# The first unit of a chunked delta rule: the inverse applied chunk by chunk inside the recurrence, with a new table of ranks

## The chip, the core and the metric

The kernel runs on one core of a Trainium2 chip. The metric is the device time of one execution in microseconds (us); lower is better. The time before is the median of four runs.

## What is computed

The input is a delta rule (linear attention with a correcting update) followed by a mixer. There are B=4 batches, H=8 heads, S=768 steps and head size D=48; everything is float32.

```python
for t in range(S):                      # per batch and head; k_n is k divided by its norm
    y[t]  = q[t] @ state
    state = state + beta[t] * outer(k_n[t], v[t] - k_n[t] @ state)
x = y, heads side by side               # (4, 768, 384)
u = x + (V^T U^T x, along the sequence) # U is 768x32, V is 32x768
out = u + relu(u @ w_ch1) @ w_ch2       # w_ch1 384x1536, w_ch2 1536x384
```

## The kernel before

**Units and chunks.** The sequence is cut into chunks of 64 steps. A unit is half of one batch: six chunks for all eight heads. There are eight units, n = 0 to 7, and batch b owns units 2b and 2b+1. Two large buffers (`slot`) hold alternate units: `kn` (k), `kq` (k and q turned, so that D lies on partitions), `pg` (first the products k k^T, later the inverse, then called `zt`), `qk` (masked q k^T), `vn` (v, in the room that q had) and `kz` (another copy of half of k).

**A unit's steps.** `load` brings k, q, v and z in by DMAs of 72 KB, four for each four heads (L383); v can only be loaded when q of the same unit has been turned, as it takes q's room. `grams` turns k and q on TensorE (L479), copies them out (L494) and forms the products (L506; masks at L537). `norms` takes the root on ScalarE (L445), forms the coefficients on VectorE (L448 to L453), and at L462 multiplies v by the norms, once v has landed. `blocks` inverts the triangular matrices: a transpose (L588), a multiply (L592), a substitution of many short VectorE instructions (L597, L603), a transpose back (L610), and `joins`, small matmuls that put the parts together (L653, L667, L693 to L714, with VectorE at L619 and L671). `diagonals` writes the result into `pg` (L732). `prepare` then forms, for three chunks at a time, (Z K)^T in the place of K^T (L812, copied by ScalarE at L831) and Z v in the place of v (L823, copied at L836). Z is the inverse.

**The recurrence.** `recur(b)` goes through the twelve chunks of a batch in order. For each chunk: TensorE multiplies (Z K) by the state (L861), VectorE subtracts that from Z v, which gives z (L874), TensorE forms K^T z (L889), and VectorE adds it to the state (L899). `outputs` forms q times the state (L776) and adds the masked product with z (L790), and ScalarE copies the result into `X` (L760).

**The mixer.** When all of a batch is in `X`, `front` forms the low-rank part (L1184, L1201) and turns the tokens (L1209). `wide` is the two large products, L1296 for w_ch1 and L1336 for w_ch2, with seven products in the place of eight by the scheme that needs sums of weights and of hidden values (L929, L1259). The last batch's first product is in `quick` (L1089). The weights arrive as pairs of 32-bit words and VectorE converts them in 14 slices, five instructions each (`load_weights`, L993 to L1021), with one ScalarE instruction between (L978).

**The order of the work.** The kernel is written as many generators ("parts"). Each yields its steps one at a time, with the engine and an assumed cost. While the kernel is built, the planner `run` keeps an assumed clock for each engine and takes one step after another; among the steps that could start within a small `hold` of the earliest one, it takes the one with the lowest rank. Each engine's instructions run on the chip in the order so written. The ranks have defaults in the code (recurrence of batch 0: 1; `norms`, `grams` and `blocks` of unit 0: 10, of unit 1: 14; `load_weights`: 40; `wide`: 95), and the table `PLACES` replaces some of them. The ranks were found by a search; they are no property of the computation. The four pairs of PSUM banks (`pair`) are handed out by the planner too, and two of the pairs go over to one bank each for the mixer when batch 0 is nearly done.

A matmul instruction of float32 appears in the profile as two records, so eight matmuls are 16 records.

Of the kernel before, what the change touches and what calls it, by code (L numbers as in the profile page):

```python
# [8 lines left out]
FP32 = mybir.dt.float32  # L9
# [17 lines left out]
def kernel(  # L27
# [20 lines left out]
    nc = tc.nc  # L48
# [61 lines left out]
    def need(*keys):  # L110
        return [key for key in keys if key[1] >= 0]
# [26 lines left out]
            waits[i] = s  # L138

    PLACES = """  # L140
    add_up b1 i0 15.701; block b0 i0 c0 64.5; block b0 i1 c2 71.091; block b0 i1 c3 56.313
    block b0 i2 c5 93.473; block b1 i0 c0 14.618; block b1 i0 c1 14.618; block b1 i1 c2 14.618
    block b1 i1 c3 14.618; block b1 i2 c4 14.618; block b1 i2 c5 14.618; block b2 i0 c0 93.5
    block b2 i0 c1 93.5; block b2 i1 c2 93.5; block b2 i1 c3 93.5; block b3 i0 c0 65.835
    block b3 i0 c1 65.835; block b3 i2 c4 65.835; block b3 i2 c5 65.835; blocks n0 1.5
    blocks n3 97.0; blocks n5 79.5; diagonals n1 h0 59.5; front b1 i0 79.5
    front b2 i0 58.8; gather b0 i0 h1 c0 70.591; gather b0 i1 h1 c0 70.591; gather b0 i1 h1 c1 70.591
    gather b1 i0 h1 c1 79.0; gather b1 i2 h1 c0 97.0; gather b2 i0 h0 c0 21.0; gather b2 i1 h1 c0 21.0
    gather b2 i1 h1 c1 21.0; grams n2 i0 81.482; grams n2 i1 89.482; grams n3 i0 20.0
    grams n5 i0 31.5; grams n5 i1 20.5; grams n7 i0 13.5; joins n1 h0 12.5  # L150
    joins n2 h0 -3.0; joins n2 h1 -3.0; joins n7 h0 106.5; joins n7 h1 102.5
    last_sum b0 i0 74.5; last_sum b2 i0 27.644; load n0 namev halves(0, 1) 74.591; load n1 namek halves(0, 1) 49.32
    load n1 nameq halves(0, 1) 49.32; load n1 namez halves(0, 1) 49.82; load n4 namek halves(0, 1) 86.5; load n7 namek halves(0, 1) 75.587
    load_beta u0 14.5; load_weights 68.5; norms n1 59.3; norms n2 81.804
    norms n7 91.523; outputs b0 c2 3.5; outputs b0 c4 76.5; outputs b0 c6 46.644
    outputs b0 c7 36.586; outputs b0 c9 90.5; outputs b1 c11 9.0; outputs b1 c5 57.185
    outputs b2 c0 37.5; outputs b2 c11 37.5; outputs b2 c5 37.5; outputs b3 c5 79.0
    placed n6 i1 j0 6.5; prepare n2 h1 5.0; prepare n3 h1 37.477; products n0 i0 j1 58
    products n0 i1 j1 58; products n1 i0 j0 81.119; products n2 i0 j1 3.5; products n2 i1 j0 76.0
    products n3 i0 j0 66.5; products n3 i0 j1 21.301; products n4 i1 j0 58.0; products n5 i1 j0 79.5  # L160
    products n5 i1 j1 79.5; products n6 i1 j0 53.243; products n6 i1 j1 70.0; products n7 i1 j0 87.58
    recur b2 46.313; recur b3 72.5; relu b0 i1 60.403; relu b1 i2 23.537
    wide b0 i0 81.619; wide b0 i1 92.619; wide b2 i1 103
    """
    PLACES = dict(x.strip().rsplit(" ", 1) for x in PLACES.replace("\n", ";").split(";") if x.strip())

# [42 lines left out]
    def run():  # L209
        stall = {}  # L210
        while waits or woken:
            while woken:
                i = woken.pop(0)
                at = max([0.0] + [done[x] for x in asked[i]])
                if at > ready[i]:
                    last[i] = None
                advance(i, None, max(at, ready[i]))
            some = {}
            for i, s in waits.items():
                e, was = s["e"], last.get(i)  # L220
# [12 lines left out]
            picks = []  # L233
            for e, them in some.items():
                soon = min(at for at, _ in them)
                them.sort(key=lambda x: (not waits[x[1]]["rush"], x[1]))
                for at, i in them:
                    hold = 0.5 if i[0] < 13 else HOLD if i[0] < 90 else SWITCH
                    if at > soon + hold:
                        continue  # L240
                    if not any(a < at and a + waits[x]["cost"] < at + 0.05 for a, x in them):
                        picks.append((at, i))
                        break
            at, i = min(picks)
            at -= stall[i]
            s, got = waits[i], None
            if s["take"]:
                banks, of = places(s)
                got = min(of, key=lambda y: (banks[y], y))
                del banks[got]  # L250
# [31 lines left out]
    def half(i, size=L):  # L282
        return slice(L * i, L * i + size)
# [81 lines left out]
    def load(n, name, halves):  # L365
# [7 lines left out]
            e = "sp" if halves == (0,) else "act"  # L373
        else:
            e = "sp"
        queue = dict(sp=nc.sync, act=nc.scalar)[e]
        for g in halves:
            if n >= NU and g:
                queue = nc.gpsimd
            for s in range(1, 4, 2) if name == "z" else range(4):  # L380
                to = dict(k=s, q=s, v=s % 2 * 2 + s // 2, z=s // 2)[name]
                yield op(e, 0.65, port=False)
                queue.dma_start(  # L383
                    out=t[half(1 - g if name == "z" else g), :, to, 0:D],
                    in_=src[b, 4 * g + s, hf * UC * L : (hf + 1) * UC * L, :].rearrange(
                        "(c t) d -> t c d", t=L
                    ),
                )
                after = landing(384)
                if name == "z" or s % 2:  # L390
                    emitted((name, n, g, s // 2), after)
# [173 lines left out]
    def blocks(n):  # L565
# [179 lines left out]
        yield need(*[(x, n, h) for x in ("upper", "diagonal") for h in range(2)])  # L745
        emitted(("joined", n))

    def recur(b):
        heads = [(j, par, g) for j in range(2) for par, g in QUADS]
        x = X[:, b % 2]  # L750
# [2 lines left out]
        def states(t):  # L753
            return t.rearrange("p g (j d) -> p g j d", j=2)
# [48 lines left out]
        def prepare(n, h):  # L803

            kn, kq, zt, _, _, vn, _, _ = units[n]
            yield need(("upper", n, h), ("diagonal", n, h), ("grams", n), ("scaled", n))
            cs = range(3 * h, 3 * h + 3)
            x = yield op("pe", 0.7, "Q", take="pair", words=96, flow=0.48)
# [38 lines left out]
        for c in range(NC):  # L847
# [3 lines left out]
            if cu == UC - 1:  # L851
                begin(outputs(c, s_old), 2 if b == 0 else 60)
                yield need(("y1", b, c))
            if c == 0:
                zs[c] = vn[:, cu]
                emitted(("b", b, c))
            else:
                xb = yield op("pe", 0.24, "Q", take="pair", words=32, flow=0.12)
                p_b = pair(xb)[:, :, 0 : 2 * D]
                for j, par, g in heads:  # L860
                    nc.tensor.matmul(  # L861
                        states(p_b)[half(g ^ par), par, j],
                        kq[half(par, D), cu, j, 0, half(g)],
                        states(s_old)[half(par, D), g, j],
                        start=True,
                        stop=True,
                    )
                emitted(("b", b, c))
                if cu < UC - 1:
                    begin(outputs(c, s_old), 2 if b == 0 else 60)  # L870
                yield need(("y", b, c - 3)) if c > 2 else []
                yield op("dve", dve(192), give=[("pair", xb)])
                z = zs[c] = small.tile([128, 4, D], FP32, name="z", bufs=3)
                nc.vector.tensor_tensor(  # L874
                    out=z.rearrange("p (r j) d -> p r (j d)", r=2),
                    in0=vn[:, cu].rearrange("p (r j) d -> p r (j d)", r=2),
                    in1=p_b,
                    op=ALU.subtract,
                )
            emitted(("z", b, c))  # L880
            if c == 0:
                begin(outputs(c, None), 2 if b == 0 else 60)
# [518 lines left out]
```

## Time and profile before

| | us |
|---|---|
| median of 4 runs | 619.59 (617.66 to 620.51) |
| time of the profiled execution | 617.66 |
| its span in the profile | 616.0 |
| TensorE busy | 585.3 |
| TensorE weight loads busy | 502.7 |
| VectorE busy | 418.8 |
| ScalarE busy | 237.5 |
| GpSimd busy | 82.3 |
| mean granted TensorE clock | 0.939 |

PE is TensorE's matmuls, PEld its weight loads, DVE VectorE, ACT ScalarE, POOL GpSimd, SP the engine whose queue issues most DMAs. "Busy" for PE includes pipelined matmuls, so it is no measure of how much arithmetic is done. Times within the span are counted from its start. The line numbers are those of the kernel before.

### The profile page before, as it was taken

What the parts mean: (1) busy time and instruction counts of PE and PEld (TensorE: products, weight loads), DVE (VectorE), ACT (ScalarE), POOL (GpSimd) and SP (SyncE); (2) the same over time, 40 slices, a digit from 0 to 9 for tenths busy, and PEclk for the clock granted to TensorE, in tenths of its full rate; (3) what the DMA queues carried; (4) which work ended last, traced back from release to release, by engine and by line L of the source; (5) the groups of instructions that cost most, each with busy time, mean ns of one, the idle gap of its engine ahead of it and who ended that gap; (6) DMA issues with size and microseconds to landing.
All of it is one profiled execution on the core that took longest, in us unless ns stands there. A gap on an engine that the chain in (4) does not pass through costs nothing.

```text
span 616.0 us, 23345 instructions
## 1 busy us (share of the span) xinstructions
PE 585.3 (95%) x10452; PEld 502.7 (82%) x10452; DVE 418.8 (68%) x1012; ACT 237.5 (39%) x474; POOL 82.3 (13%) x145
## 2 busy tenths in 40 slices
PE   6588978999999999999999999999999999999997
PEld 5588977789888778799889888888889868755997
DVE  5879997898989713888898527898886125332542
ACT  3465565740342563421530744245324431344000
POOL 3011052410010342300100510501001000000000
PEclk9766565999999999999999999999999999999999
DMA  8840567850000241410000610510000000000000
GB/s 152 155 89 5 179 179 169 186 133 14 15 4 29 57 84 39 75 54 0 29 4 2 125 41 11 128 28 3 29 2 2 29 4 1 26 1 0 13 33 33
DMA packets 72292, 33.26 MB, mean 54 GB/s; under 512 B 59648, under 2 KB 70656, under 8 KB 72192
## 3 DMA queue, kind: packets, MB, share of 16 engines
q1 hardware_dynamic: 66400, 24.98, 18.2%
q0 software_dynamic: 4192, 6.49, 4.7%
q8 instruction: 82, 1.34, 0.9%
q10 hardware_dynamic: 1600, 0.30, 0.3%
q14 instruction: 18, 0.15, 0.1%
HBM read 27.03 MB, written 4.72 MB: 52 GB/s over the span
## 4 chain that ended last, share of the span: by engine, by line
PE 84%; DVE 6%; SPq 5%; issue 2%; ACT 1%; DMA 1%; DVEq 0%; ACTq 0%
PE P L1336 27%; PE P L1296 24%; PE P L1089 7%; SPq L383 5%; PE P L506 3%; PE P L861 2%; PE P L1201 2%; PE P L479 2%; PE P L812 2%; PE P L823 2%; PE P L776 2%; PE P L889 2%; PE P L790 2%; PE P L667 1%; PE P L1184 1%
## 5 line engine op out<-in xcount | busy, mean ns | idle before, releaser
L1296 PE MATMUL P<-ut,w_sb 128*128 128x256 f32 x648 | 154.8, 387 | 0.0
L1296 PEld LDWEIGHTS P<-ut,w_sb 128*128 128x128 f32 x648 | 118.4, 190 | 17.0 <-issue 0.6
L1336 PE MATMUL P<-w_sb,hs 128*128 128x192 f32 x540 | 95.4, 330 | 0.0
L1336 PEld LDWEIGHTS P<-w_sb,hs 128*128 128x128 f32 x540 | 87.6, 190 | 3.8 <-issue 1.2
L1239 ACT ACTIVATE hs<-P 128x512 f32<-128x512 f32 x54 | 32.3, 598 | 97.8 <-PE P L1296 93.7
L603 DVE TENSOR_TENSOR xt<-xt,prod 128x112 f32<-128x112 f32 (+21 forms) x200 | 64.6, 323 | 6.9
L1272 DVE TENSOR_TENSOR X<-X,P 128x192 f32<-128x192 f32 x84 | 29.5, 351 | 56.5 <-PE P L1336 56.0
L597 DVE TENSOR_TENSOR prod<-gs,xt 128x112 f32<-128x112 f32 (+21 forms) x200 | 64.1, 321 | 4.8
L760 ACT COPY X<-P 64x192 f32<-64x192 f32 x96 | 30.1, 313 | 72.4 <-PE P L790 55.8
L1336 PE MATMUL P<-w_sb,S 128*128 128x192 f32 x288 | 50.5, 329 | 0.0
L1336 PEld LDWEIGHTS P<-w_sb,S 128*128 128x128 f32 x288 | 46.8, 190 | 0.6
L479 PE MATMUL P<-ident,slot 128*128 128x128 f32 x192 | 30.3, 309 | 14.7 <-DMA slot<-in_k_dram 11.1
L874 DVE TENSOR_TENSOR z<-slot,P 128x192 f32<-128x192 f32 x44 | 15.5, 352 | 41.2 <-PE P L861 40.5
L479 PEld LDWEIGHTS P<-ident,slot 128*128 128x128 f32 x192 | 25.0, 159 | 19.7 <-issue 15.8
L732 ACT COPY slot<-zz 32x384 f32<-32x384 f32 x64 | 32.5, 509 | 11.5 <-DVE zz L610 7.9
L494 ACT COPY slot<-P 128x768 f32<-128x768 f32 x30 | 23.7, 802 | 31.5 <-PE P L479 31.3
L1089 PE MATMUL P<-slot,w_sb 128*128 128x384 f32 x96 | 33.2, 486 | 0.0
L582 POOL MEMSET xt<- 128x1056 f32 x8 | 7.8, 980 | 186.2 <-DVE zz L610 186.2
L506 PE MATMUL P<-slot 48*64 48x64 f32 x1536 | 31.8, 238 | 0.5 <-ACT slot L494 0.2
L506 PEld LDWEIGHTS P<-slot 48*64 48x64 f32 x1536 | 28.7, 150 | 3.9 <-ACT slot L494 2.0
L1336 PE MATMUL P<-w_sb,slot 128*128 128x192 f32 x180 | 30.1, 326 | 0.0
L1336 PEld LDWEIGHTS P<-w_sb,slot 128*128 128x128 f32 x180 | 29.4, 190 | 0.5
(143 smaller groups left out, 911.5 us busy)
## 6 DMA issues: line engine op xcount, KB each, us to landing
out_dram<-X SPq DMA_DIRECT2D x22, 192.0 KB, 1.9
slot<-in_k_dram SPq DMA_DIRECT2D x56, 72.0 KB, 4.7
X<-in_moe_w_ch_dram SPq DMA_DIRECT2D x10, 384.0 KB, 5.2
wide<-in_moe_w_ch_dram SPq DMA_DIRECT2D x10, 384.0 KB, 4.4
slot<-in_q_dram SPq DMA_DIRECT2D x40, 72.0 KB, 3.9
slot<-in_v_dram SPq DMA_DIRECT2D x40, 72.0 KB, 3.2
slot<-in_k_dram POOLq DMA_DIRECT2D x36, 72.0 KB, 4.3
slot<-in_q_dram POOLq DMA_DIRECT2D x24, 72.0 KB, 4.8
```

Source lines behind the costliest of these rows:

```text
L383: queue.dma_start(out=t[half(1 - g if name == "z" else g), :, to, 0:D], in_=src[b, 4 * g + s, hf * UC * L : (hf + 1) * UC * L, :].rearrang ...
L479: nc.tensor.transpose(p_t[:, c // 3, c % 3], t[:, c, 2 * j : 2 * j + 2].rearrange("p s d -> p (s d)"), ident,)
L506: nc.tensor.matmul(p_g[half(g ^ (par * i)), par, c], kq[rows, c, j, 0, half(g)], kq[rows, c, j, i, half(g)], start=True, stop=True,)
L597: nc.vector.tensor_tensor(out=prod, in0=gb[:, :, j : j + 1, j + 1 :].to_broadcast([128, split, m, w]), in1=xb[:, :, 0:m, j : j + 1].to_bro ...
L603: nc.vector.tensor_tensor(out=xb[:, :, 0:m, j + 1 :], in0=xb[:, :, 0:m, j + 1 :], in1=prod, op=ALU.subtract,)
L732: nc.scalar.copy(pg[quarter(i), :, at, :, a : a + BK], cut(zc, h)[quarter(i)].rearrange("p r (c j) t -> p r c j t", j=2),)
L760: nc.scalar.copy(x[half(c % 2), c // 2, 4 * D * g : 4 * D * (g + 1)].rearrange("p (j r d) -> p r j d", r=2, d=D), states(p_y)[half(g)],)
L1089: nc.tensor.matmul(to, w, t, start=start, stop=stop, skip_group_check=True)
L1239: nc.scalar.activation(hs[:, fs[0] : fs[1] + 1 : fs[1] - fs[0]], p_f, ACTF.Relu)
L1272: nc.vector.tensor_tensor(out=to, in0=to, in1=p, op=ALU.add)
L1296: nc.tensor.matmul(p_f[:, fs.index(f)], w1_sb[:, y, 256 * t + 128 * fs.index(f) :][:, 0:128], ut[:, t], start=(t == 0), stop=(t == KT - 1),)
L1336: nc.tensor.matmul(p_o, a[:, f], w2_sb[:, w, f], start=(first and f == 0), stop=(f == HF - 1), skip_group_check=True,)
```

## The change

For units listed in `DIRECT`, here only unit 0, `prepare` issues nothing: it waits for the same four results and declares the unit ready. K^T stays in `kq` and v, times its norms, stays in `vn`. In the recurrence, a chunk of unit 0 first multiplies K by the state, subtracts this from v in place, and then multiplies by the inverse with eight more matmuls into a PSUM pair of their own, which ScalarE copies out as z. Chunk 0 has no state yet, so it has the added product alone.

```diff
+    DIRECT = (0,)
 def prepare(n, h):
+            if n in DIRECT:
+                yield need(("upper", n, h), ("diagonal", n, h), ("grams", n), ("scaled", n))
+                emitted(("ready", n, h))
+                return
 def recur(b):
+            def solved():
+                x = yield op("pe", 0.24, "Q", take="pair", words=32, flow=0.12)
+                p_z = pair(x)[:, :, 0 : 2 * D]
+                for j, par, g in heads:
+                    nc.tensor.matmul(
+                        states(p_z)[half(g ^ par), par, j],
+                        units[n][2][half(g), par, cu, j],
+                        vn[half(g), cu, 2 * par + j],
+                        start=True, stop=True,
+                    )
+                yield op("act", act(192), give=[("pair", x)])
+                zs[c] = small.tile([128, 4, D], FP32, name="z", bufs=3)
+                nc.scalar.copy(zs[c].rearrange("p (r j) d -> p r (j d)", r=2), p_z)
+            if c == 0 and n in DIRECT:
+                emitted(("b", b, c))
+                yield from solved()
-            if c == 0:
+            elif c == 0:
                 zs[c] = vn[:, cu]
...
-                    states(p_b)[half(g ^ par), par, j],
+                    states(p_b)[half(g if n in DIRECT else g ^ par), par, j],
...
                 nc.vector.tensor_tensor(           # v minus K state, in place for unit 0
-                    out=z ...
+                    out=(rows if n in DIRECT else zs[c]) ...
+                if n in DIRECT:
+                    yield from solved()
```

The table of ranks is replaced as a whole, with 75 entries in the place of the old ones. Those that the prediction speaks of, with the value before (the default where the table had none):

| step | rank before | rank after |
|---|---|---|
| load of k, unit 1 | 49.32 | 11 (default) |
| load of z, unit 1 | 49.82 | 16 (default) |
| load of q, unit 0 | 12 (default) | 69.54 |
| load of q, unit 1 | 49.32 | 97.22 |
| load of v, unit 0 | 74.591 | 15 (default) |
| load of weight slice 1 (the next ones follow it) | 22 (default) | 126.08 |
| `norms`, unit 0 | 10 (default) | 79.64 |
| `norms`, unit 1 | 59.3 | 26.1 |
| `load_weights` (the conversion) | 68.5 | 43.83 |
| `joins` of unit 1, first half | 12.5 | 39.0 |
| `prepare` of unit 1, second half | 3 (default) | 65.74 |
| `diagonals` of unit 1, both halves | 59.5; 14 (default) | 71.0; 85.0 |
| `outputs` of batch 0, chunks 2, 3 and 4 (the state step of a chunk waits for the first half of its `outputs`) | 3.5; 2 (default); 76.5 | 86.0 each |
| `recur` of batch 1 | 59 (default) | 5.5 |

Two small edits in the planner go with it. The `hold` for steps with ranks under 13 goes from 0.5 to 0.35. And the half of a later unit's loads that goes out on the GpSimd queue is now also charged to that queue's assumed clock, where it was charged to SP's; the queue that issues it is the same.

More of the change, by code (lines that the diff above doesn't have):

```diff
@@ L140 @@
     PLACES = """
[L141 to L163, printed above, removed]
+    add_up b0 i0 31.92; add_up b0 i1 69.89; block b0 i1 c2 30.5; block b0 i1 c3 30.5
@@ new lines @@
+    block b0 i2 c4 30.5; block b0 i2 c5 95.19; block b1 i2 c4 44.55; block b1 i2 c5 56.39
+    blocks n3 93.5; blocks n5 10.25; blocks n6 108.22; diagonals n1 h0 71.0
+    diagonals n1 h1 85.0; diagonals n3 h1 2.0; diagonals n5 h1 28.38; front b0 i0 66.59
+    gather b1 i0 h0 c0 80.14; gather b1 i0 h0 c1 82.14; gather b2 i0 h1 c1 31.0; grams n2 i0 4.0
+    grams n5 i0 21.85; joins n1 h0 39.0; joins n2 h1 76.87; joins n3 h1 39.0
+    joins n4 h0 13.0; joins n4 h1 13.0; joins n5 h0 36.42; joins n5 h1 8.5
@@ new lines @@
+    joins n7 h1 82.5; load n0 nameq halves(0, 1) 69.54; load n1 nameq halves(0, 1) 97.22; load n2 namev halves(0, 1) 69.5
+    load n3 nameq halves(0, 1) 38.0; load n4 nameq halves(0, 1) 80.57; load n4 namez halves(0, 1) -9.78; load n5 namek halves(0, 1) 83.0
+    load n7 namez halves(0, 1) 97.07; load_beta u0 42.08; load_beta u1 86.0; load_weights 43.83
+    norms n0 79.64; norms n1 26.1; norms n3 43.6; norms n4 100.22
+    norms n7 25.88; outputs b0 c10 49.59; outputs b0 c2 87.0; outputs b0 c3 86.0
@@ new lines @@
+    outputs b0 c4 86.0; outputs b0 c9 63.51; outputs b1 c5 32.92; outputs b2 c0 89.0
+    outputs b2 c5 56.14; outputs b3 c0 73.14; outputs b3 c1 72.14; outputs b3 c6 73.14
+    prepare n1 h1 65.74; prepare n5 h0 40.99; prepare n5 h1 40.99; products n0 i0 j0 79.64
+    products n0 i0 j1 81.64; products n0 i1 j1 80.64; products n1 i1 j1 39.92; products n2 i0 j1 88.0
+    products n2 i1 j0 16.07; products n2 i1 j1 99.72; products n3 i1 j1 -2.55; products n4 i1 j0 70.79
+    products n4 i1 j1 70.14; products n6 i0 j0 2.37; recur b1 5.5; relu b0 i0 90.0
@@ L164 @@
+    start i1 126.08; start i9 6.0; weight_sums 30.62
     """
@@ L237, in run @@
                 for at, i in them:
-                    hold = 0.5 if i[0] < 13 else HOLD if i[0] < 90 else SWITCH
+                    hold = 0.35 if i[0] < 13 else HOLD if i[0] < 90 else SWITCH
                     if at > soon + hold:
@@ L375, in load @@
             e = "sp"
-        queue = dict(sp=nc.sync, act=nc.scalar)[e]
         for g in halves:
             if n >= NU and g:
-                queue = nc.gpsimd
+                e = "pool"
+            queue = dict(sp=nc.sync, act=nc.scalar, pool=nc.gpsimd)[e]
             for s in range(1, 4, 2) if name == "z" else range(4):
@@ L853, in recur @@
                 yield need(("y1", b, c))
-            if c == 0:
+            def solved():
[6 more added lines that the diff above has]
+                        vn[half(g), cu, 2 * par + j],
+                        start=True,
+                        stop=True,
+                    )
[6 more added lines that the diff above has]
+            elif c == 0:
                 zs[c] = vn[:, cu]
@@ L872, in recur @@
                 yield op("dve", dve(192), give=[("pair", xb)])
-                z = zs[c] = small.tile([128, 4, D], FP32, name="z", bufs=3)
+                rows = vn[:, cu]
+                if n not in DIRECT:
+                    zs[c] = small.tile([128, 4, D], FP32, name="z", bufs=3)
                 nc.vector.tensor_tensor(
-                    out=z.rearrange("p (r j) d -> p r (j d)", r=2),
-                    in0=vn[:, cu].rearrange("p (r j) d -> p r (j d)", r=2),
+                    out=(rows if n in DIRECT else zs[c]).rearrange("p (r j) d -> p r (j d)", r=2),
+                    in0=rows.rearrange("p (r j) d -> p r (j d)", r=2),
                     in1=p_b,
```

## The prediction

> **What bounds the kernel now.** I read the busy time by stretches first. The columns are: length, then PE, PEld, DVE, ACT and POOL busy with their instruction counts, granted clock, DMA share, GB/s.
>
> ```profile
> 0.00:35.40 35.40, 21.87 (x456) 19.64 (x457) 26.66 (x82) 16.59 (x31) 6.11 (x17) 0.88 0.82 146
> 35.40:39.40 4.00, 4.00 (x80) 4.00 (x80) 0.01 (x1) 2.78 (x8) 0.00 (x0) 0.50 0.50 91
> 39.40:64.50 25.10, 21.38 (x750) 19.79 (x750) 23.61 (x65) 15.41 (x32) 2.63 (x5) 0.57 0.14 26
> 64.50:106.00 41.50, 35.50 (x1126) 32.84 (x1124) 36.89 (x62) 22.63 (x46) 12.16 (x20) 0.54 0.70 183
> 106.00:144.00 38.00, 37.91 (x441) 30.42 (x435) 33.79 (x54) 20.81 (x33) 9.16 (x14) 0.96 0.64 142
> 144.00:529.00 385.00, 380.95 (x7248) 330.14 (x7247) 268.18 (x691) 139.26 (x286) 52.21 (x89) 1.00 0.15 33
> ```
>
> There are two regimes. From 106 to the end TensorE is full: 4.05 us free in 385. That part is a fixed amount of matmul work, so whatever start-up loses or wins is passed on to the end. Before 106, batch 0 goes through its inverse and recurrence while VectorE also converts the weights. From 39.4 to 144, VectorE is busy 23.61 + 36.89 + 33.79 = 94.3 of 104.6 us (90%), and TensorE 94.8 at mostly half clock. So VectorE has little room to make up a hole, and just ahead of this stretch lies the hole of the second row: 0.01 us of work in 4.00. The timeline of VectorE shows what it is.
>
> ```profile
> 35.09 0.27 DVE L429 STREAM_TRANSPOSE betas<-beta_rows 128x128 f32<-128x128 f32 x1
> 39.40 1.36 DVE L462 TENSOR_TENSOR slot<-slot,norm_rows 128x1152 f32<-128x1152 f32 x1 [4.03 <-DMA slot<-in_v_dram]
> ...
> 43.92 0.69 DVE L592 TENSOR_TENSOR gs<-gs,cp 128x512 f32<-128x512 f32 x1
> ```
>
> L462 is v of unit 0 times its norms. It stands at the head of VectorE's queue and waits 4.03 us for v; unit 1's inversion (L592 and the substitution) stands behind it. The chain of waits goes through the same place, back along the SP queue, which issues the loads one by one at 0.62 us each, to the start of the run:
>
> ```profile
> 35.15 0.62 SPq L383
> 35.77 0.04 issue
> 35.81 3.26 DMA slot<-in_v_dram
> ```
>
> **The step that is removed.** `prepare` of unit 0 has 4 x 24 matmuls, two records each. Its TensorE time from 45 to 60, for L812 and then for L823:
>
> ```profile
> 45.00:60.00 15.00, 3.64 (x96) 3.18 (x96) 0.61 0.02 5
> 45.00:60.00 15.00, 3.27 (x96) 3.11 (x96) 0.61 0.02 5
> ```
>
> That is 3.64 + 3.27 = 6.91 us. On ScalarE two copies of 0.80 (L831) and two of 0.64 (L836) go: 2.88 us.
>
> **The step that is added.** Six groups of eight matmuls, 64x64 weights by 64x48. L790's product with z has this shape; the added copy moves 128x192, as L701 does.
>
> ```profile
> 62.66 0.64 PE L790 MATMUL P<-z,slot 64*64 64x48 f32 x16
> 50.70 0.32 ACT L701 COPY zz<-P 128x192 f32<-128x192 f32 x1 [0.52 <-PE P L696]
> 82.67 0.41 PE L790 MATMUL P<-z,slot 64*64 64x48 f32 x16
> ```
>
> At half clock that is 6 x 0.64 = 3.84 us on TensorE and 6 x 0.32 = 1.92 us on ScalarE. The balance is -3.07 us of TensorE, -0.96 of ScalarE, and nothing on VectorE (the subtraction stays, only its output moves).
>
> On the chain of unit 0's recurrence the group, the copy and two hand-overs of about 0.07 (L790's end at 63.30 to ScalarE's start at 63.37) make 1.1 us per chunk, 6.6 in all. Against that, `prepare` no longer stands ahead of chunk 0 (L812 at 46.57 to L836's end at 50.19: 3.6) and of chunk 3 (54.99 to 59.02: 4.0, partly beside chunks 0 to 2). Unit 0's chain thus changes by between -1.0 and +3.0.
>
> Neither is on the path now. z of chunk 4 is written at 64.5, yet its state product starts only at 77.2: 12.7 us of cover, in which TensorE does unit 1's joins (L653, L667). Unit 1 is ready at 81.2, and its first chunk starts at 83.5. I take 0 for this, with -3.07 (all the TensorE time saved) and +3.0 as bounds; if the cover is gone, the rival below gives the price. The eight matmuls also wait on ScalarE's FIFO with z: behind a copied chunk stands at most one conversion instruction L978 of 0.94, inside the same cover.
>
> [...] From 64.5 to 77.2 TensorE is busy 12.15 of 12.70 us, with a granted clock of 0.50; from 50.5 to 55.5 it is busy 2.96 of 5.00, with 0.84. So density alone does not raise the clock in these rows, and I leave the price at half clock. [...]
>
> **The ranks.** On SP, k and z of unit 1 (12 DMAs) now go ahead of q of unit 0, and v of unit 0 no longer waits behind q of unit 1. By ranks: 4 k, 8 k, 8 z at 0.67 us (0.62 and 0.04 between) puts q of unit 0 at 14 to 20; q of unit 1 fills SP while q of unit 0 lands and is turned; then v goes out to about 31 and lands, with 3.3 more, at about 34, where it was 39.07. The weights' slice 1 goes behind that, but was converted only from 60.9. And `norms` of unit 0 (rank 79.64, L462 with it) now stands behind unit 1's inversion (14) and norms (26.1) on VectorE. Either alone takes the 4.03 us away.
>
> What is late next is the root of unit 1's norms, which ended at 39.44, behind the copies L530 of k's products:
>
> ```profile
> 39.20 0.24 ACT L445 ACTIVATE norm<-gs 128x32 f32<-128x32 f32 x1
> ```
>
> If that stays, the substitution still starts 43.92 - 39.44 - 1.2 (norms, L448 to L453) = 3.3 us earlier. But k of unit 1 is now issued from 3.8 instead of 14.4, which takes L530's copies away from that place. VectorE's displaced 1.36 + 0.54 + 0.58 + 0.98 (L462 to L537) must still be done, so VectorE wins no more than its hole: 4.0, with 3.3 as the lower end.
>
> All ranks past 144 are new as well. No row shows their order. The free TensorE time there is 4.05 us, so I bound them by -4.05 and +4.05 and take 0.
>
> **The sum.** 617.66 (the profiled execution; span 616.0 and 1.66 around it) - 4.0 = 613.7. The median lies 1.93 above the profiled execution, so 615.6. The forecast's own range is 3.3 to 7.1 less: 612.5 to 616.3.
>
> **Rivals.** *Slower: unit 0's recurrence becomes the path.* Now its state after chunk 5 is there at 83.0, just when unit 1 wants it. With the wait gone, the substitution ends at 51.6, and if L462 comes after it and the transpose (2.1), v is scaled at 51.6 + 2.1 + 1.4 = 55.1. Chunks were 3.0 us apart alone (L889 at 59.35 and 62.31) and 4.0 with others about (L874 from 84.08 to 104.22, five steps); with 1.1 each that is 4.1 or 5.1. Six chunks end at 79.7 or 85.7. The turning point is (83.0 - 55.1)/6 = 4.65 us per chunk. Above it the time is longer than before, by 2.7 us at 5.1; if the wait for v stays too, v is scaled at 59.0, chunk 5 ends at 89.6, and it is 6.6. The middle, +4.6, is 624.2. For it: `outputs` of chunks 2, 3 and 4 now have rank 86, behind unit 1's joins (39) and preparation (1 and 65.74), and the state step waits for them; each chunk also needs one more PSUM pair of four. Against it: the 12.7 us of cover, and six joins groups that fit into waits of a chain now longer.
>
> *No change: the hole moves.* The planner has once put L462 4.03 us ahead of its data; a wait of the same size for the weights, whose slice 1 now goes out last on SP, or the order of ranks not moving L462 at all, takes the gain back. VectorE's 10 free us from 39.4 to 144 could hold it. Time: 617.5 to 620, say 619.
>
> *Faster still.* TensorE's 3.07 us were on the path after all, through the joins of unit 1 that run beside, and half of the 4.05 us later is won: 615.6 - 3.1 - 2.0 = 610.5.
>
> **Chances.** Forecast 0.36, faster still 0.12, no change 0.22, slower 0.30. A measurement of this kernel can tell about 0.5% (3.1 us) from no change; the forecast lies 0.64% below, so some of its chance falls within: of 0.36, 0.05. That gives faster 0.43, same 0.27, slower 0.30. The range takes in the fast rival less part of the unknown ranks, 609, and most of the slow one, 625.
>
> **What would show it.** VectorE's idle row before L462 is gone or under 1 us, and L592 of unit 1 starts near 38 to 40 in the place of 43.92. L812 and L823 have 96 records fewer each, and six groups of 16 new ones with a ScalarE copy of 0.32 lie before 80. The first L1296 starts near 116 in the place of 120.0, and the last conversion sum (L929) ends near 140 in the place of 143.8. The prediction is wrong if the first chunk of unit 1 starts later than 83.5 because it waits for L899 of chunk 5, or if VectorE shows a new idle row of several us before 100.

## The result and the profile after

| | before | after |
|---|---|---|
| median, us | 617.92 (79 runs, 614.32 to 623.24) | 620.48 (53 runs, 615.46 to 624.35) |
| time of the profiled execution, us | 617.66 | 618.58 |
| its span, us | 616.0 | 616.9 |
| TensorE busy, us | 585.3 | 583.3 |

The ratio is 1.0038, with a 95% interval of 1.0025 to 1.0051: 2.6 us slower, where 2.3 us faster than 617.92 stood in the prediction. By the bound of 0.5% this is no change, but the sign is settled and it is the other one. 620.48 lies inside the wide range of 609 to 625, outside the forecast's own of 612.5 to 616.3.

The stretches of the kernel after, with the columns of those shown before (length; PE, PEld, DVE, ACT and POOL busy; granted clock; DMA share; GB/s):

```profile
0.00:35.40 35.40, 24.81 (x508) 22.45 (x508) 26.15 (x80) 19.75 (x38) 6.08 (x17) 0.91 0.69 116
35.40:39.40 4.00, 4.00 (x134) 3.82 (x134) 3.76 (x8) 2.57 (x6) 0.41 (x1) 0.50 0.63 111
39.40:64.50 25.10, 20.70 (x580) 19.18 (x579) 21.42 (x60) 10.19 (x23) 2.22 (x5) 0.50 0.24 65
64.50:106.00 41.50, 31.43 (x1025) 28.50 (x1025) 34.78 (x59) 23.30 (x45) 10.69 (x17) 0.57 0.70 179
106.00:144.00 38.00, 36.63 (x471) 29.95 (x466) 35.29 (x56) 21.21 (x37) 10.87 (x18) 1.00 0.67 147
144.00:529.00 385.00, 381.12 (x7288) 329.91 (x7285) 268.55 (x691) 139.75 (x286) 51.81 (x89) 1.00 0.16 32
```

Read TensorE's idle time, length less PE, beside the rows of before. Up to 39.4 it falls from 13.53 to 10.59: the early gain of 2.9 us came. From 39.4 to 106 it rises from 9.72 to 14.47: 4.75 us are lost again. From 106 to 144 it rises by 1.28, and after that the two are alike within 0.2. With 1.98 us less of PE's work in the whole span this makes the 0.9 us by which the spans differ. (The two profiled executions are 0.9 us apart, the medians 2.6: the profile shows part of the loss.)

VectorE's timeline shows what became of the hole (L458 was L462, L588 was L592, L667 was L671, L897 was L874):

```profile
35.54 0.54 DVE L667 SCALAR_TENSOR_TENSOR zz<-P,upper_rows,zz 128x96 f32<-128x96 f32 x2 [1.76 <-issue]
...
36.86 1.36 DVE L458 TENSOR_TENSOR slot<-slot,norm_rows 128x1152 f32<-128x1152 f32 x1
...
41.42 0.68 DVE L588 TENSOR_TENSOR gs<-gs,cp 128x512 f32<-128x512 f32 x1
...
48.66 0.35 DVE L897 TENSOR_TENSOR slot<-slot,P 128x192 f32<-128x192 f32 x1 [0.83 <-PE P L882]
53.58 0.35 DVE L897 TENSOR_TENSOR slot<-slot,P 128x192 f32<-128x192 f32 x1 [0.69 <-PE P L882]
```

L458 hardly waits (v landed at 36.8, not at about 34 as forecast), and 1.76 us of idle time before L667 stand where 4.03 stood. L588 starts 2.5 us earlier. But now L897 of unit 0 stands inside unit 1's substitution and waits there for TensorE's product with K (L882), so the substitution ends only 0.9 us earlier (56.9 for 57.8).

And TensorE's own waits from 39 to 106, line by line, those that the profile puts down to no releaser ("issue"; total, times, longest), of the kernel after:

```profile
PE P L914 <- issue: 3.3, 2, 1.9
PE P L882 <- issue: 1.9, 2, 1.4
PE P L825 <- issue: 0.3, 1, 0.3
```

and of the kernel before:

```profile
PE P L790 <- issue: 1.3, 1, 1.3
PE P L776 <- issue: 0.5, 1, 0.5
PE P L711 <- issue: 0.2, 1, 0.2
```

These are waits for no engine and no load: 5.5 us after, 2.0 before. The difference, 3.5 us, is most of the 4.75 that are lost there. My prediction has no term for it, though the source has one: the planner `run` counts the instructions of each matmul group in lots (`LOT`, 256) and charges at least 4.1 us (`FETCH`) from one lot to the next, an assumed figure (r16 below measured 3.45 to 4.55). The waits stand at fixed places: if TensorE's matmul and weight-load records are counted from the start, those over 0.4 us begin at records 1702, 1956, 3996 and 4252 in the kernel after and 3999 and 4254 in the kernel before, all a few records from a multiple of 256 plus 160. The list of DMA queues in the profile's page has the one that goes with it (packets, MB, share of 16 engines):

```profile
q8 instruction: 81, 1.33, 0.9%
```

1.33 MB in 81 packets are 16.4 KB each, and 20,712 TensorE records over 81 are 256. (In the kernel before, 82 packets, 1.34 MB, go with 20,904 records.) So in these traces TensorE's instructions come in lots of 256, and the change moves the limits of all later lots: it removes 384 instructions and adds 192 (each float32 matmul is two loads and two matmuls: the 48 of L812 were 96 records of each).

### The profile page after: what moved, and what is told of

Its sections match the earlier page's. It is cut to its first block, busy times and chain, and to the rows that moved or that the text cites. A ratio compares the mean times of both kernels' runs of the same rounds, so it can differ in the third digit from the quotient of the medians.

```text
span 616.9 us, 23144 instructions
## 1 busy us (share of the span) xinstructions
PE 583.3 (95%) x10356; PEld 500.6 (81%) x10356; DVE 419.3 (68%) x1012; ACT 236.2 (38%) x476; POOL 82.1 (13%) x145
## 3 DMA queue, kind: packets, MB, share of 16 engines
q8 instruction: 81, 1.33, 0.9%
## 4 chain that ended last, share of the span: by engine, by line
PE 83%; DVE 8%; SPq 4%; issue 2%; DMA 2%; ACT 1%; DVEq 0%; ACTq 0%
PE P L1361 26%; PE P L1321 23%; PE P L1114 7%; SPq L379 4%; PE P L502 3%; PE P L882 3%; PE P L475 2%; PE P L1226 2%; PE P L914 2%; PE P L649 2%; PE P L663 2%; PE P L774 1%; PE P L788 1%; DMA slot<-in_k_dram 1%; PE P L814 1%
## 5 line engine op out<-in xcount | busy, mean ns | idle before, releaser
L379 POOL DMA_DIRECT2D slot<-in_k_dram x36 | 23.3, 658 | 83.2 <-PE P L914 67.4
L897 DVE TENSOR_TENSOR z<-slot,P 128x192 f32<-128x192 f32 x39 | 13.8, 353 | 23.5 <-PE P L882 22.8
L490 ACT COPY slot<-P 128x768 f32<-128x768 f32 x30 | 23.6, 800 | 14.6 <-PE P L475 14.3
```

The source lines that it names most:

```text
L379: queue.dma_start(out=t[half(1 - g if name == "z" else g), :, to, 0:D], in_=src[b, 4 * g + s, hf * UC * L : (hf + 1) * UC * L, :].rearrang ...
```

## The experiments

Theories. **Lots:** the gain forecast was there, and the shifted lots take it back. **Step:** the longer chain of unit 0 costs by itself. **Ranks:** the new order is what costs. In all experiments the order of the steps is written out as a list, taken from the kernel before or from the kernel after, in the place of the planner's choices, so that an edit moves nothing else; the lines shift a little. All but the last were timed in 4 to 12 executions each. Each ratio is to the kernel before on the same chip (618.2 to 618.6 us).

### The move of v's norms alone: r2_v_scaled_later

```diff
 # order of before
-VectorE: L462 of unit 0 ahead of unit 1's norms
+VectorE: L462 of unit 0 behind L592 of unit 1
```

> The kernel before in its frozen order with one instruction moved: L462, v of unit 0 times the norms, goes from the head of VectorE's queue to behind L592 of unit 1. No other order changes. The prediction's sum (the hole of 4.03 us is passed on to the end): 3.3 to 4.0 us faster, 0.9935 to 0.9947. Theory C (what follows 64 us is set by TensorE's chain of joins, preparation and recurrence, not by VectorE's total): the hole closes, unit 1's substitution ends 2 to 4 us earlier, and the end moves by less than 1.5 us.

617.79 us, ratio 0.9979 (0.9956 to 1.0001): 1.3 us by the ratio, 0.5 by the medians, not 4.0; the end moves by less than 1.5 us, as theory C had it. It is the fastest kernel run, though its interval just touches no change. VectorE's timeline (L637 is before's L671, L558 is L592, L428 is L462):

```profile
42.63 0.54 DVE L637 SCALAR_TENSOR_TENSOR zz<-P,upper_rows,zz 128x96 f32<-128x96 f32 x2 [6.68 <-ACT norm L411]
...
45.88 0.68 DVE L558 TENSOR_TENSOR gs<-gs,cp 128x512 f32<-128x512 f32 x1
46.48 1.35 DVE L428 TENSOR_TENSOR slot<-slot,norm_rows 128x1152 f32<-128x1152 f32 x1
```

The wait for v is gone, and the next instruction in VectorE's queue is as late: the subtraction in unit 0's joins, which needs TensorE's joins. (The profile names ScalarE's root, which ended at 42.51. TensorE's L633, which L637 reads, runs from 39.81 to 43.8, and the 48 records read first end at 42.53, so the two are equally late.) In the kernel before this instruction stood hidden behind L462, at 40.67.

This profile is of the slowest of r2's twelve executions (621.11), in which TensorE's joins ran 3.1 us later than in the profile before, so it shows the order of the waits and not what they are worth. r10 below has the same move, and its profiled execution (624.36) lies near its median (624.91). Its VectorE timeline (L653 is before's L671, L574 is L592):

```profile
39.59 0.54 DVE L653 SCALAR_TENSOR_TENSOR zz<-P,upper_rows,zz 128x96 f32<-128x96 f32 x2 [4.01 <-ACT norm L427]
...
42.84 0.68 DVE L574 TENSOR_TENSOR gs<-gs,cp 128x512 f32<-128x512 f32 x1
```

A wait of 4.01 us stands there in the place of 4.03, and L592's counterpart starts 1.1 us earlier (42.84 for 43.92), which is near the gain of 1.3.

### The direct form alone: r1_direct_alone, r9_direct_aligned, r13_direct_idle_fill

```diff
 # order of before; the added product and copy of a chunk right behind its subtraction
+    DIRECT = (0,)
```

> Every instruction in the order of the kernel before, frozen; only unit 0 is made direct: its preparation is gone, and the added product and copy stand right behind each chunk's subtraction (for chunk 0 where the preparation stood). Theory A (the step itself is about free, as predicted: 12.7 us of cover): within 1 us of before, 0.998 to 1.002. Theory B (unit 0's longer chain reaches the path): 2 to 5 us slower, 1.003 to 1.008.

627.53 us, ratio 1.0146 (1.0120 to 1.0173), above both forecasts. This mixes the step with shifted lots. r9 and r13 put the lots back with 48 matmuls of 32 x 32 x 32 on the identity, 192 instructions, whose results nobody reads. In r9 they stand in the recurrence:

```diff
 def solved():
     ...                                   # the eight added matmuls
+    for _ in range(24 if c in (0, 2) else 0):
+        nc.tensor.matmul(pair(x)[0:32, 1, 480:512], ident[0:32, 0:32], ident[0:32, 0:32], ...)
```

> The kernel before in its own frozen order with unit 0's direct form, as in r1_direct_alone, plus 24 matmuls of 32 x 32 x 32 on the identity behind the added products of chunk 0 and 24 more behind those of chunk 2. They put back the 192 TensorE instructions that the form leaves out (384 removed, 192 added), so that from chunk 5 on every lot of 256 instructions begins where it does in the kernel before; they cost some 48 x 2 x 56 ns = 5.4 us of TensorE's time, which with 6.91 removed and 3.84 added makes 2.3 us more TensorE work than before. Theory (the loss of r1_direct_alone, 627.5 us and ratio 1.0146, was the shifted lots alone, and the step itself is about free): 617.5 to 621.5, ratio 0.998 to 1.005. Rival (the step's longer chain of unit 0, some 1.1 us per chunk in r1_direct_alone, is what costs): 625 to 630, ratio 1.011 to 1.018, whatever the lots.

625.87 us, ratio 1.0105 (1.0080 to 1.0130), in the rival's range. 1.7 us less than r1, although 48 matmuls were added, and they stand in the recurrence, on the path that is measured. In r13 they stand where TensorE is idle:

```diff
+for i in range(8): nc.tensor.matmul(...)          # at the start
 def turn(t, j, i):
+    for _ in range(40 if (n, i, j) == (1, 0, 0) else 0):
+        nc.tensor.matmul(...)                      # ahead of the first transposes of unit 1's k
```

> As r9_direct_aligned (the kernel before in its frozen order with unit 0's direct form, lots put back by 48 matmuls of 32 x 32 x 32), but with the 48 where they lie on no chain: 8 at the start and 40 ahead of the first transposes of unit 1's k, where TensorE stands idle from 18.9 to 24 us. If the step itself lengthens unit 0's chunks (1.1 us for c2 and 1.5 us for c3 in r1_direct_alone) and unit 1's joins behind them: 622.5 to 626, ratio 1.007 to 1.013. If r9_direct_aligned's 7.6 us were its own 48 matmuls and the step is free: 617.5 to 620.5, ratio below 1.004.

623.26 us, ratio 1.0093 (1.0069 to 1.0118), and in its profile no wait for instructions from 39 us on. So **the step by itself costs 5.1 us in the order before**, with the added group right behind each subtraction; up to 1.1 us of it may be the filling, which is what r11 below loses with 40 of its 64 matmuls at the same place. TensorE's timeline, first of the kernel before:

```profile
63.44 0.68 PE L861 MATMUL P<-s,slot 48*64 48x48 f32 x16
63.90 0.64 PE L790 MATMUL P<-z,slot 64*64 64x48 f32 x16
64.33 2.72 PE L653 MATMUL P<-zz,hs 64*64 64x16 f32 x48
```

then of r13 (L872 is the product of K with the state, L851 the added product, L904 K^T z, L639 before's L653):

```profile
59.65 0.68 PE L872 MATMUL P<-s,slot 48*64 48x48 f32 x16 [1.80 <-DVE s L914]
60.84 0.68 PE L851 MATMUL P<-slot 64*64 64x48 f32 x16 [0.51 <-DVE slot L887]
...
65.31 0.68 PE L851 MATMUL P<-slot 64*64 64x48 f32 x16 [0.23 <-DVE slot L887]
66.41 0.57 PE L904 MATMUL P<-z,slot 64*48 64x48 f32 x16 [0.43 <-ACT z L860]
...
69.21 2.75 PE L639 MATMUL P<-zz,hs 64*64 64x16 f32 x48
```

TensorE stands idle for each hand-over of the longer chain, and **unit 1's joins, queued behind chunks 1 to 4 of unit 0 in TensorE's order, start 4.9 us later** (69.21 for 64.33). Of these, 1.1 were there before the recurrence: in this execution v was scaled at 40.47 for 39.40. The steps from one state to the next grew, for chunks 1 to 5, by 0.6, 0.8, 1.6, 0.9 and 1.3 us, 5.2 in all.

### Both, in the order before: r10_direct_aligned_v_later

This is r9 with r2's move.

> r9_direct_aligned and, with it, the move of r2_v_scaled_later (unit 0's norms on v behind the copy of unit 1's blocks). If the two are independent: r9_direct_aligned less 1.3 us, the gain that the move had by itself. If the direct form takes over the wait that the move frees, no difference from r9_direct_aligned within 0.6 us. Were r9_direct_aligned at the kernel before, this would be near 617, the best so far beside r2_v_scaled_later's 617.8.

624.91 us, ratio 1.0090 (1.0059 to 1.0121): 0.96 below r9. The point estimate is near r2's 1.3, but the intervals overlap too much to tell it from no gain.

### The ranks alone: r3_ranks_alone, r12_ranks_aligned

```diff
 # order of after; prepare of unit 0 put in at chunks 0 and 3
-    DIRECT = (0,)
+    DIRECT = ()
```

> The changed kernel's frozen order without the direct unit: the added products and copies are taken out and unit 0's preparation is put back, the first half ahead of chunk 0 and the second ahead of chunk 3. Theory D (the new order costs the time, the step is free): like the changed kernel, 1.002 to 1.006 of before. Theory B (the step costs it): faster than the changed kernel by 2 us or more, 0.995 to 1.000 of before.

628.5 us, ratio 1.0157 (1.0119 to 1.0195), above both forecasts. This adds 192 instructions to the kernel after; r12 adds 16 matmuls (64 instructions) behind the preparation of chunks 3 to 5, which makes it a whole lot:

> The kernel after in its own frozen order with unit 0's preparation put back, as in r3_ranks_alone (628.5 us, ratio 1.0157), plus 16 matmuls of 32 x 32 x 32 behind the preparation of chunks 3 to 5, which make the 192 instructions that this adds to the kernel after a whole lot of 256. Theory (the step is about free and the lots set the rest): near the kernel after, 618.5 to 623, ratio 1.000 to 1.008. Rival (the order after needs the direct form, and is worth 10 us less without it): 626 to 631, ratio 1.012 to 1.02.

623.78 us, ratio 1.0083 (1.0054 to 1.0112), so **the new order without the step costs 5.5 us, with waits for instructions of its own** (5.5 us in its profile, 2.2 in that of the kernel before). In this run VectorE's subtraction for chunk 3 also waits 3.7 us for the preparation with the 16 added matmuls, so part of the price may be the place where the preparation was put back; no other place was tried. Together, step and order cost 2.6, not 10.6. The reading that fits: the order puts unit 1's joins ahead of chunks 3 and 4 of unit 0, which the step makes longer (chunk 3's state is ready at 67.1 in the kernel after, 63.4 before), so the longer chain no longer holds up the joins. That this is the whole of it was not shown. (r12 fell between its two forecasts.) In the kernel after, the joins of unit 1 (L649, L663) run from 57.6 on, and chunk 3's K^T z (L914) comes at 66.0, behind most of them.

### Moving the lots: r4 to r8, r11, r14, r15

Each adds matmuls of 32 x 32 x 32 on the identity, whose results nobody reads, and nothing else:

```diff
     nc.vector.memset(P[:, :, 0:256], 0.0)
+    for i in range(N):
+        nc.tensor.matmul(P[0:32, 7, 480:512], ident[0:32, 0:32], ident[0:32, 0:32], start=True, stop=True)
```

N is 8, 16, 24 or 32. In r11 24 stand there and 40 in the idle time ahead of the first transposes of unit 1's k; in r15 16 there and 24 in the idle time ahead of the first transposes of unit 0's q. Start-up hides 16 of them, and 32 put TensorE's next work back by up to 0.6 us in the profile.

> The changed kernel in its frozen order, with 32 tiny matmuls (128 TensorE instructions, into an unused corner of PSUM) ahead of all work, while TensorE waits for the first data. TensorE's instructions then reach the queue in lots cut 128 instructions earlier. Theory E (the waits of 1.9 and 1.4 us without a releaser at 91.6 and 98.5, and 1.4 at 46.6, come where a lot of instructions is fetched, and where they fall is luck): these waits move to other instructions, and the time changes by 1 to 3 us, most likely down. Theory D (the order itself): no change from the changed kernel beyond 0.5 us.

> The changed kernel in its frozen order with 16 tiny matmuls (64 TensorE instructions) ahead of all work; in the run with 32 they started at 3.2 us and took 56 ns each record, so 16 fit ahead of the first data at 5.4. The profiles show TensorE's waits without a releaser at instruction numbers that leave 156 to 166 when divided by 256, in every kernel so far; their sum was 1.85 us before, 5.5 in the changed kernel and 8.2 with 128 instructions ahead. Theory F (the changed order wins 2.9 us of TensorE idle time up to 39 us, and loses it to these waits): the time follows the sum of these waits, so a shift with a sum of 2 to 3 gives 2 to 3 us less than the changed kernel, and one with 8 gives 3 to 5 more. Theory D (the order itself costs it): the time is that of the changed kernel within 1 us, whatever the sum.

> The same with 24 tiny matmuls (96 instructions), about 0.2 us of them beyond the arrival of the first data. Theory F: the time follows the sum of the waits at lot ends as in the run with 64. Theory D: within 1 us of the changed kernel.

> The kernel before in its frozen order with 16 tiny matmuls (64 instructions) ahead. Theory F applies to this order too: its 1.85 us of waits at lot ends is a favourable place of the lots, so another place gives 4 to 8 us of waits and a time 2 to 6 us above before, 1.003 to 1.010. Theory G (the order before is insensitive; only the changed order is fragile): within 1 us of before.

> The kernel before with 32 tiny matmuls (128 instructions), which cost some 0.5 us at the start. Theory F: 2 to 6 us above before, as the changed kernel lost some 5 us by the same shift. Theory G: within 1 us of before.

> The kernel before in its frozen order with 64 matmuls of 32 x 32 x 32 added, 24 at the start and 40 ahead of the first transposes of unit 1's k, where TensorE stands idle from 18.9 to 24 us: 256 instructions, one whole lot, twice what r8_before_shift128 added (635.3 us, ratio 1.028). If what those shifts cost is where the lots of 256 end, a shift by a whole lot puts them back, except near the start: 618 to 620.5, ratio 0.999 to 1.004. Rival (the added work or its place costs, not the lots): at least as slow as the shift by 128, 635 or more.

> The kernel after in its frozen order with 8 matmuls of 32 x 32 x 32 at the start (32 instructions). Theory (where the lots end sets its waits for instructions, 5.5 us before 106 us in the kernel after): the time goes with the sum of those waits in its own profile; 615 to 618 if the sum falls under 3 us, 622 to 630 if it rises over 7. Rival (the order, not the lots, has lost the early gain): within 1 us of 620.5 whatever that sum.

> The kernel after in its frozen order with 16 matmuls of 32 x 32 x 32 at the start and 24 ahead of the first transposes of unit 0's q, where TensorE stands idle from 19.5 to 22.3 us (160 instructions). The same two expectations as for r14_after_shift32: 615 to 618 with under 3 us of waits for instructions, 622 to 630 with over 7; or within 1 us of 620.5 whatever they are.

The waits for instructions are TensorE's waits with no releaser from 39 to 640 us, summed over lines, each from one profiled execution, whose time stands beside them.

| kernel | shift, instructions | median us | ratio to before | waits for instructions, us | profiled execution, us |
|---|---|---|---|---|---|
| before | 0 | 617.92 | 1 | 2.2 | 617.66 |
| r7 | 64 | 627.89 | 1.0138 (1.0105 to 1.0171) | 8.8 | 629.71 |
| r8 | 128 | 635.33 | 1.0282 (1.0243 to 1.0322) | 12.4 | 636.81 |
| r11 | 256 | 619.32 | 1.0019 (1.0001 to 1.0037) | 3.0 | 620.12 |
| after | 0 | 620.48 | 1.0038 (1.0025 to 1.0051) | 5.5 | 618.58 |
| r14 | 32 | 619.14 | 1.0019 (0.9992 to 1.0046) | 4.7 | 617.39 |
| r5 | 64 | 619.49 | 1.0020 (0.9997 to 1.0043) | 6.9 | 625.53 |
| r6 | 96 | 629.89 | 1.0181 (1.0147 to 1.0215) | 7.1 | 626.40 |
| r4 | 128 | 625.84 | 1.0118 (1.0095 to 1.0140) | 10.1 | 625.61 |
| r15 | 160 | 629.42 | 1.0165 (1.0135 to 1.0195) | 14.6 | 630.80 |

r8 and r11 decide it for the order before. 32 added matmuls, 3.6 us of TensorE in time that is mostly idle (64 records of 56 ns), make the kernel 17 us slower; twice as many, a whole lot, make it 1.1 us slower. What costs is where the lots end. A place in r8 where time is lost after 144 us, by stretches (length, PE busy, granted clock, DMA share, GB/s) and in TensorE's timeline:

```profile
167.00:169.10 2.10, 0.31 (x16) 0.91 0.00 0
169.10:172.00 2.90, 2.90 (x38) 0.50 0.03 6
```

```profile
167.00 0.31 PE L651 MATMUL P<-zz 32*32 32x16 f32 x16
169.10 0.62 PE L651 MATMUL P<-zz 32*32 32x16 f32 x32 [1.79 <-issue]
```

In the middle of a group of small matmuls TensorE stands for 1.79 us with the DMAs idle (share 0.00), and the clock granted for the 2.9 us that follow is 0.50.

The waits go with the time of the execution that they were read from: those with at most 5.5 us of them took 617.4 to 620.1 us, those with 6.9 or more 625.5 to 636.8. (r5's profile is of its slowest execution, 6.0 us above its median.) They are not the whole account: r8 lost 17 us with 10.2 more of them. As for the expectations, r11 and r15 came out as the lots have it. r7 and r8 lost more than the 2 to 6 us expected, r4 went up by 5.4 us where down was thought likelier, and r6 by 9.4. r5's median stayed within 1 us of the kernel after, as its rival has it, and r14 fell between its two forecasts. No shift of the kernel after had under 4.7, so whether its order beats the kernel before without these waits was not shown.

The granted clock is a rival that no run set apart. Its mean over an execution has a median of 0.939 in the kernel before, 0.934 in the kernel after and 0.930 to 0.932 in r1, r8 and r13; r11 has 0.939. A difference of 0.005 is some 6 us of 618 at 0.50 in the place of 1.00, worth up to 3 us of TensorE's work, as much as the loss of 2.6; both figures are estimates from these means. Whether the waits bring the lower clock or the lower clock comes by itself is open.

### The supply by itself: r16_supply

```diff
 # order of before; at the start 1024, at the end 512 of
+    rows = slice(32 * (i % 4), 32 * (i % 4) + 32)
+    nc.tensor.matmul(P[rows, 7, 496:512], ident[rows, rows], ident[rows, rows.start : rows.start + 16], ...)
```

> The kernel before in its frozen order with 1024 matmuls of 32 x 32 x 16 on four places of the array in turn ahead of everything on TensorE, and 512 more behind everything; 4096 and 2048 instructions, 16 and 8 lots. In the kernel before, matmuls of this shape ran at 10 ns a record (116 in 1.18 us), so a lot needs some 1.3 us of TensorE. Theory (a lot comes no sooner than 3.3 us after the one ahead of it when the DMAs are idle, 4.7 to 7.4 us when they load): after the lots that are there from the start, TensorE waits at every lot; one lot per 4.7 to 7.4 us before 35 us, 3.3 us per lot later on and at the end. Rival (the waits have another cause and only fall at these places): 1.3 to 2 us per lot throughout, and no waits, so the first group ends before 35 us.

One execution, with a span of 697.9 us. TensorE's timeline, three rows of the group at the start and one of that at the end:

```profile
12.74 1.90 PE L299 MATMUL P<-ident 32*32 32x16 f32 x128 [2.37 <-issue]
...
47.12 1.90 PE L299 MATMUL P<-ident 32*32 32x16 f32 x128 [1.55 <-issue]
50.85 1.90 PE L299 MATMUL P<-ident 32*32 32x16 f32 x128 [1.83 <-issue]
```

```profile
681.62 1.90 PE L1387 MATMUL P<-ident 32*32 32x16 f32 x128 [1.84 <-issue]
```

Every row is 128 matmul records, and 128 loads: one lot, 1.90 us of work, then a wait. Lots follow each other by 3.45 to 4.00 us with the DMAs quiet (share 0.02) and 4.00 to 4.55 in the first 25 us, most of it with loads (share 0.81 up to 20). The theory holds (3.45 us at the least, for its 3.3), its loaded figure (4.7 to 7.4) was too high here, and the rival is out: it had no waits. (In the trace of the kernel after, q8's packets start 3.34 us apart at the least, and 3.84 to 7.40 from 59.7 to 108.5.) The first wait is at record 446, behind 223 matmuls and as many loads, so at most two lots were there ahead. A lot per 3.6 us is 14 ns an instruction.

## Why the prediction was wrong, step by step

**The hole.** Right as an event: L462's wait is gone, and TensorE had 2.9 us less idle time by 39.4. Wrong in two places. The lower end of 3.3 us let unit 1's norms start when the root was done. But L671, L619 and L537 (0.54, 0.58 and 0.98 us) stand between in VectorE's queue, and L671 waits for TensorE until the root is done too: r10 has its counterpart at 39.59, and 1.1 us are won, not 3.3. And a win at 39.4 was passed on whole to the end because VectorE is 90% busy from there to 144. But up to 106 the gain still had to pass TensorE's order, with 9.72 us of idle time in it that could grow, and it grew. The term of -4.0 measured -1.3 where it stands alone (r2, with an interval that touches 0).

**The step.** "I take 0" failed: it measured +5.1 in the order before (r13). The 12.7 us of cover were there for z of chunk 4, as read, but they were made of work that stands *behind* chunks 1 to 4 in TensorE's queue. On the engine that carries the longer chain this was no cover: each wait in the chain pushed it back. The bound of +3.0 put on the chain was too low as well, since the 3.6 us of `prepare` ahead of chunk 0 had stood inside a wait for VectorE: TensorE waits 1.71 us for the first state in the kernel before and 3.42 in r13. The slower rival had the mechanism, about 1.1 us more per chunk, and 624.2 for it; r13 is at 623.3. It did not ask whether the new order makes room; in the kernel after, chunk 5's state is there at 83.2, where r13 has 89.7.

**The ranks.** "I take 0" stood for the order after 144, which was right within 0.2 us of TensorE's idle time. The order ahead of that is worth +5.5 without the step (r12) and about -2.5 with it (2.6 less r13's 5.1), both with the places of the lots mixed in. (The rank of chunk 2's `outputs` became 87.0, not 86.0, which changes nothing here.)

**Instructions.** No term at all. The step was counted in microseconds of TensorE and never in instructions, so 192 fewer of them looked like a gain only. They move every later lot. The planner does count them, so both orders were made with the lots where its assumed figures put them; I read the ranks and not that charge. The excess of waits in the kernel after, 3.3 us, is larger than its loss of 2.6, so it can account for all of it; that it does was not shown, for want of a shift without such waits. So the terms that failed are measured one by one, and the cause of the 2.6 us that remain when they meet stays open.

**The clock.** Left at half for the start, which held: 0.50 from 39.4 to 64.5 and 0.57 to 106. What makes it fall was not shown. In r8 it fell from 1.00 (166.0 to 168.7) to 0.50 (168.7 to 175.5) around a wait of 1.79 us in dense work: TensorE was busy for 6.95 of the 7.00 us from 160.0 to 167.0, and for 1.31 of the 2.70 us ahead of the fall.

**What was to be seen.** L462's wait gone: yes. L592 at 38 to 40: 41.42. First wide product near 116: 116.0. Last conversion sum near 140: it ends at 142.8, where it was 143.8, so 1.0 of the 4.0 us was kept. The six added groups before 80: five, the sixth at 80.5. First chunk of unit 1 not later than 83.5: it starts at 87.75. TensorE's timeline of the kernel before,

```profile
83.50 0.45 PE L861 MATMUL P<-s,slot 48*64 48x48 f32 x16 [0.41 <-DVE s L899]
```

and of the kernel after (L814 and L825 are the preparation of unit 1, L882 is the product with the state):

```profile
83.30 1.56 PE L814 MATMUL P<-slot 64*64 64x64 f32 x48 [0.68 <-ACT slot L716]
84.61 1.50 PE L825 MATMUL P<-slot 64*64 64x48 f32 x48
...
87.75 0.45 PE L882 MATMUL P<-s,slot 48*64 48x48 f32 x16
```

It does not wait for chunk 5's state, the sign that was named: that is there at 83.2 (83.4 before). The preparation of unit 1, which before came partly behind this chunk (86.03 and 90.88), now stands ahead of it in TensorE's queue. Chunk 8's state is level again (96.6 for 96.9); then a wait for instructions of 1.45 us stands inside the next chunk's K^T z, and chunk 9's state is at 100.7 for 99.3. VectorE's longest new idle row before 100 is 2.5 us, behind the K^T z that holds the wait of 1.9.

## What to carry to other kernels

Count instructions as well as microseconds: a stretch of small matmuls that could have taken 256 instructions in 1.90 us waited for its supply here, a lot every 3.45 to 4.55 us (r16), and the edits that changed their number moved the later waits (a sum of 2.2 us in the kernel before, 12.4 in r8); a small difference between two versions should be read at equal counts (padded in idle time to a whole lot) or at several shifts. In r13 work that stood behind the chain on the same engine did not hide it (the step cost 5.1 us): read the queue order of the engine that carries the chain before calling its busy time cover. When a wait is taken off an in-order queue, look at the release time of every instruction behind it, not only of the one that seems next on the path.

## What the runs showed of the hardware

In these traces TensorE's instructions came in lots of 256 (81 packets of 16.4 KB on q8 for 20,712 records in the kernel after; rows of 128 matmuls and 128 loads in r16), and in r16 a lot came every 3.45 to 4.55 us, slower than TensorE executed its small matmuls (1.90 us). The kernel before issues 3,738 loads and matmuls from 39.4 to 106, 14.6 lots; at 3.6 us they are 53 of 66.6 us, an estimate from r16's spacing that says how near the start-up of this kernel lies to the supply.

Waits of 1.55 to 2.65 us stand at every boundary of r16's two groups but the first of each, and in r8 a shift of the boundaries by 128 instructions went with a loss of 17 us.

In r8 a wait went with a second loss: around the one of 1.79 us the clock was 0.50 for 6.8 us (168.7 to 175.5), and its mean from 144 to 529 is 0.98, where the kernel before has 1.00. Yet in r16 the clock stayed at 1.00 from 20 to 60 us with TensorE busy for 4.78 to 5.70 of each 10 us, and was 0.50 from 680 to 690 with 4.96 of 10. What sets it was not settled, nor was why a lot takes longer in some places than in others.
